# A decay-delta attention and gated MoE kernel whose table of work order is drawn anew

## The chip, the cores and the metric

The kernel runs on one core of a Trainium2 chip. The metric is device time in microseconds (us) of one execution, the median of several runs. Lower is better. The engines of a core run side by side, each strictly in the order of its own instructions: PE is TensorE (matmuls, transposes), DVE is VectorE, ACT is ScalarE, POOL is GpSimd, and SP issues the DMAs.

## The reference

The reference has two parts. A recurrent attention over 768 steps keeps one 40 x 40 state per batch (4) and head (8):

```python
y[:, :, t] = np.einsum('bhd,bhde->bhe', rt, state)
Sa = np.einsum('bhde,bhe->bhd', state, at)
state_decay = state * wt[:, :, None, :] - np.einsum('bhd,bhe->bhde', Sa, bt)
state = state_decay + np.einsum('bhd,bhe->bhde', vt, kt)
```

Its output, turned to `x` of shape (4, 768, 320), goes through `h = relu(x @ w_in)` (320 to 1024), a convolution of three taps along the sequence, `gate = sigmoid(conv)`, and `(h * gate) @ w_out` (1024 to 320). The weights arrive as 64-bit floats.

## The kernel before

**Chunks.** The 768 steps are cut into 24 chunks of 32. Inside a chunk the recurrence becomes matrix products and the inverse of a triangular system. Two neighbouring chunks (2j and 2j+1) form pair j and share their loads (`wakb`), their decays and one solve, so there are twelve solves. All four batches stand together on the 128 partitions.

**The chain of a pair.** `scores n` makes the products of the decayed rows on PE (L411, `ps`) and masks them on DVE into `at` (L437). Once both chunks of a pair have their scores, `solve_in j` takes `at` to DRAM (`bd`, L461) and back, rearranged, as `bb` (L465). `solve j` then runs 31 iterations of two operations, a product into `st` (L480) and an addition to `xx` (L486), each needing the one before. A solve of an even j runs on DVE, one of an odd j on POOL (`VSOL`). Its last step takes `xx` to DRAM (`xd`, L491) and back as `tt` (L496), which is what PE needs in the second step of `chain 2j` and of `chain 2j+1` (`pu`, L533). Only the solve's matrix goes this way; the solves of different pairs do not depend on each other, but there is one buffer each for `xx` and `bb` (two for `tt`, three for `at`), so solves run one after the other.

**The state.** `chain n` has four steps: the product with the old state on PE (`pp`, copied by ACT into `psb`), `pu` and its copy `u`, the update `pn` on PE (L549) with the addition on DVE (`s`, L562), and the scaling by the decay on POOL (L568). Chain n needs chain n-1. From the state, `u` and the turned inputs, `pairs` and `outputs` make the chunk's result, and `finish` lays it out for the second part.

**The second part.** Two chunks make a window of 64 steps; there are twelve windows. `moe_in n.fp` (four per window, ten steps each) has two halves on PE (L700), relu on ACT, the taps on ACT and DVE (L729), sigmoid, the gate, and a split into high and low parts on ACT and POOL (L743). `moe_out n.bo` (two per window) has four quarters of six matmuls (L754). `weights i` (23 pieces) turns 64-bit weights into 32-bit pairs in eight DVE operations each (L217 to L235), spread over the first third of the program.

**What sets the order.** Nothing is reordered by a scheduler. Each kind of work is a generator that gives up control after each of its steps. A long string, `ORDER`, names which work advances next, `sc21` one step of `scores 21`, `so10*2` two steps of `solve 10`, and so on. The instructions go onto their engines' queues in this order. A step whose prerequisites (`put`) have not been emitted makes them advance first:

```python
for token in ORDER.split():
    name, _, times = token.partition("*")
    ...
        advance((KINDS[name[:2]], *numbers))
```

The two-letter names are we weights, ld wakb, de decays, dd decayed, sc scores, ha hats, si solve_in, so solve, ch chain, rt/vt/ut/st turns, pa pairs, ou outputs, fi finish, pk pack, mi moe_in, mo moe_out.

Of the kernel before, what the change touches and what calls it, by code (L numbers as in the profile page):

```python
# [31 lines left out]
)  # L32

ORDER = """
    ld0 de0.0*2 ld0*2 de0.1 ld0 ld1 de0.1 we0 dd0.0*3 dd0.1*2 sc0 dd0.1 we0 ld1*2 lr0 sc0 sc1 lr1
    de1.0 sc1 ha0 de1.0 dd1.0 de1.1*2 we1*4 si0 ha0 ha1 dd1.0 we0*2 rt0 ld1 so0 ha1 dd1.0 so0 dd1.1
    ld2 so0*2 ld2 dd1.1 ld2 so0 dd1.1 ha2*2 sc2 ld2 lv0 lv1 vt0 ha3*2 so0*3 sc2 sc3 we2*2 sc3 we3
    we2*2 we3 we4 so0 we3*2 we5 we4 we5 si1 de2.0*2 ch0*4 we4*2 we6 lv2 de2.1*2 so1*2 ld3 ut0 pa0
    vt1 dd2.0*2 de3.0 we5 so1 we5 we7 ou0 we6 fi0 so1 dd2.0 ch1 we6 dd2.1 we7*2 ch1 we7 dd2.1*2 ld3
    st1*2 sc4 we6 so1 we8*4 we9 we10 ch1 lv3 rt1 we9 st1*2 ut1 pa1 lr2 ou1 ha4 ld3*2 we10 so1*3 fi0  # L40
    vt2 we10 fi0 fi1 de3.0 sc4 sc5 we9 we10 sc5 ch1 de3.1 we9 de3.1 ha4 we11 we12 lr3 rt2 fi1 st2*2
    fi1 we11 we12 we11*2 ro0 we13 we12*2 ha5 st2 we13 we14 ha5 ld4 so1 we13 dd3.0*3 dd3.1*3 we14*2
    ch2 si2 so2 ch2 pk0 ut2 so2*2 pa2 vt3 sc6 so2*2 st2 ou2 ch2 ro0 rt3 mi0.0*3 so2*2 mi0.0*2 ch2
    st3*2 we13 mi0.1*2 st3 ld4 so2 ld4 we14 lv4 we15 we16 ch3*2 sc6 sc7 ut3 we15 st3 we15 sc7 fi2*3
    lr4 mi0.0 pa3 mi0.0 ch3 we15 ch3 we16 mi0.0 we17 mi0.1 mi0.2 we17*2 mi0.2 so2 ch4 si3 we16 so3
    ou3 ha6 we16 we18 de4.0 we18 ha6 ha7 st4 fi3*2 we17 we19 de4.0 we18 mi0.1 we19 vt4 st4*3 lv5
    de4.1 ch4 ut4 so3 ch4 dd4.0 rt4 we18 we20 de4.1 we20 mi0.2 so3 we20 pa4 vt5 ch4 ch5 so3 mi0.2
    ch5 fi3 ha7 we19*2 we21*2 ut5 we20 we22*2 ou4 st5*2 mi0.1 st5 lr5 rt5 so3 we22 ld4 ld5 de5.0
    mi0.1 we21 ch5 we22 mi0.3 we21 mi0.0*2 so3 mi0.1*2 mi0.3 pa5 mi0.3 pk1 dd4.0*2 dd4.1 mi0.1*2
    dd4.1 st5 mi0.2 sc8 fi4*2 ld5 dd4.1 ou5 mi0.2 lv6 mi0.3 so3*2 sc8 mi0.2 sc9 mi0.2*2 ha8*2 ha9  # L50
    fi4 fi5 ld5 de5.0 de5.1 ha9 sc9 mi0.2 dd5.0 mi0.3 dd5.0 de5.1 lv7 mi1.0*3 mi1.1 ld5 dd5.0 dd5.1
    sc10 so3 si4 mi0.3 lr6 dd5.1*2 ch5 mi0.3 lr7 mi0.3 mi1.1*2 mi1.0*3 mi1.1 mi1.2 vt6 sc10 mi0.3
    mo0.0 sc11 mi0.3 mi1.1 mi1.0*2 mi1.1 ch6 st6 mi1.2 ch6*2 sc11 mi1.1*2 mo0.0*2 ch6 mo0.0 mo0.1*5
    ld6 ut6 rt6 ch7 mi1.1 so4 ld6 so4*2 pa6 vt7 st6 fi5*2 st6 so4*2 mi1.0 so4 mi1.2 st6 mi1.3 so4
    mi1.2 so4 lv8 ou6 mi1.0 mo1.0 mi1.2 mi1.3*2 st7*2 ch7 ut7 mi1.1 st7*2 rt7 ch7*2 mo1.0 pa7
    mi1.3*2 fi6*2 pk2 lr8 mi1.2*2 ou7 mi1.2 rt8 so4 si5 ch8 st8*2 mi1.2 mi1.3 mi1.2 mi1.3 ch8*2 lv9
    fi6 mi2.0*2 lr9 ld6 ch8 ha10*2 fi7 mi1.3*2 ha11 ld6 de6.0 vt8 lv10 de6.0 dd6.0 fi7 mi2.0 mi1.3
    mi2.1 ch9 mo1.0 mi2.0*2 de6.1 ch9 de6.1 so5*2 mi2.1 so5 mi2.0 ut8 mi2.1*4 mi2.0 mo0.0 mo1.0*2
    mo1.1 ha11 mi2.0 mi2.1 mo1.1 dd6.0 mo1.1 dd6.0 pa8 vt9 mo1.1 mi2.0*2 dd6.1 so5 fi7 st8*2 mi2.1*2
    dd6.1 so5 ou8 rt9 mi2.2 sc12 mi2.2*2 mi2.3*3 ut9 dd6.1 st9 mi2.1 mi2.2 ch9 mi2.2 mi2.3*2 mi2.2*2  # L60
    ld7 de7.0 lr10 ld7*2 so5*3 pa9 ch9 lr11 st9*3 pk3 ld7 mi2.3 mi2.2 mi3.0*2 mi2.3 mi3.0 mi2.3 fi8
    so5 fi8 mi2.2*2 mi2.3 mi3.0 ou9 mi3.1 fi8 sc12 fi9 de7.0 dd7.0 sc13 mo2.0*2 sc13 de7.1*2 mi3.1*2
    rt10 ha12*2 ha13 dd7.0 ha13 dd7.0 mi2.3 mi3.0 dd7.1*3 ch10 mi3.1*2 mi3.0 mi3.1 st10 fi9 mo2.0*2
    mo2.1 ch10*3 mo2.1 mi3.0 st10 mi3.1 st10*2 mi3.0 mi3.1 ut10 si6 so6 mi3.2*2 so6 lv11 vt10 mi3.2
    pa10 vt11 so6 mo1.1 so6 mi3.3 mo2.1 mi3.3 ch11 mo2.0 mo2.1 ld8 mi3.0 lr12 so6 ch11 so6 ou10 rt11
    mi3.3 mi3.1 ut11 pa11 st11*3 ld8 lv12 so6 mi3.2 mi3.3 st11 so6 sc14 ch11 vt12 mi3.1 lr13 sc14
    mi3.0 mo3.0 mi3.2 sc15 mi3.2 ch11 mi3.2 fi9 fi10 mi3.3 fi10*2 ou11 st12 ha14 sc15 mi3.2*2 mi3.3
    pk4 so6 ch12 mi3.2 de8.0 mi4.0*2 mi3.3 fi11*2 mi3.3 ch12*2 mo3.0 mi3.3*2 ch12 mi4.0*2 ut12 si7
# [934 lines left out]
```

## Time and profile before

| what | value |
|---|---|
| time, median of 3 runs | 711.0 us (708.99 to 714.0) |
| the profiled execution | 708.08 us |
| its span in the trace | 706.4 us (1.7 us of the time lie outside it) |
| mean granted TensorE clock | 0.906 of full speed |
| busy: PE / DVE / POOL / ACT | 560.7 / 538.4 / 353.2 / 350.7 us |

The span is cut into forty slices, whose digits are the busy tenths of each engine. A group's row gives line, engine, operation, its output and inputs, its count, its busy time and the mean of one, and how long the engine was idle ahead of it, with what ended that. A row of the timeline gives start, duration and the operation. A row of the waits gives total time, number of waits and the longest.

### The profile page before, as it was taken

What the parts mean: (1) busy time and instruction counts of PE and PEld (TensorE: products, weight loads), DVE (VectorE), ACT (ScalarE), POOL (GpSimd) and SP (SyncE); (2) the same over time, 40 slices, a digit from 0 to 9 for tenths busy, and PEclk for the clock granted to TensorE, in tenths of its full rate; (3) what the DMA queues carried; (4) which work ended last, traced back from release to release, by engine and by line L of the source; (5) the groups of instructions that cost most, each with busy time, mean ns of one, the idle gap of its engine ahead of it and who ended that gap; (6) DMA issues with size and microseconds to landing.
All of it is one profiled execution on the core that took longest, in us unless ns stands there. A gap on an engine that the chain in (4) does not pass through costs nothing. (4 is left out here: it accounts for less than half of the span.)

```text
span 706.4 us, 29930 instructions
## 1 busy us (share of the span) xinstructions
PE 560.7 (79%) x13021; PEld 497.9 (70%) x13021; DVE 538.4 (76%) x1261; ACT 350.7 (50%) x792; POOL 353.2 (50%) x582
## 2 busy tenths in 40 slices
PE   4444764677687898988977996899998977899886
PEld 3334654566576787977866885789887876788775
DVE  6689889998999896657795578987979894456571
ACT  2322244254375455664454664466565546455651
POOL 2001884037786235783234884236985028863321
PEclk9766777997799998989999998999998999999998
DMA  8765456437125344544404446524435025121000
GB/s 139 120 117 108 103 112 102 95 94 144 22 41 107 56 72 79 94 81 82 82 20 89 86 86 106 81 60 69 89 62 91 6 54 94 29 51 32 21 30 19
DMA packets 242402, 53.40 MB, mean 76 GB/s; under 512 B 229000, under 2 KB 238112, under 8 KB 242272
## 3 DMA queue, kind: packets, MB, share of 16 engines
q1 hardware_dynamic: 242272, 51.50, 39.9%
q8 instruction: 102, 1.67, 1.0%
q14 instruction: 28, 0.23, 0.1%
HBM read 38.63 MB, written 10.22 MB: 69 GB/s over the span
## 5 line engine op out<-in xcount | busy, mean ns | idle before, releaser
L729 DVE SCALAR_TENSOR_TENSOR cc<-hb,cw,cc 128x256 f32<-128x256 f32 x192 | 106.3, 575 | 13.7 <-ACT cc L721 10.2
L568 POOL TENSOR_TENSOR s<-s,wc 120x360 f32<-120x360 f32 x88 | 75.8, 891 | 69.4 <-DVE s L562 69.4
L486 POOL TENSOR_TENSOR xx<-xx,st 128x126 f32<-128x126 f32 (+22 forms) x186 | 83.1, 447 | 14.6
L480 POOL TENSOR_TENSOR st<-xx,bb 128x126 f32<-128x126 f32 (+22 forms) x186 | 79.4, 427 | 21.1 <-DMA bb<-bd 8.4
L700 PE MATMUL ph<-xh,wih 120*128 120x256 f32 x288 | 56.6, 306 | 11.3 <-ACT hb L714 11.3
L486 DVE TENSOR_TENSOR xx<-xx,st 128x126 f32<-128x126 f32 (+22 forms) x186 | 54.2, 291 | 6.4
L480 DVE TENSOR_TENSOR st<-xx,bb 128x126 f32<-128x126 f32 (+22 forms) x186 | 53.6, 288 | 7.2 <-DMA bb<-bd 1.7
L736 DVE TENSOR_TENSOR cc<-cc,hb 128x512 f32<-128x512 f32 x48 | 40.8, 857 | 21.7 <-ACT cc L734 21.5
L562 DVE TENSOR_TENSOR s<-pn,s 120x360 f32<-120x360 f32 x88 | 40.6, 522 | 20.6 <-PE pn L549 20.6
L700 PEld LDWEIGHTS ph<-xh,wih 120*128 120x128 f32 x288 | 41.8, 194 | 15.0 <-ACT hb L714 13.1
L734 ACT ACTIVATE cc<-cc 128x512 f32<-128x512 f32 x48 | 30.4, 636 | 43.6 <-DVE cc L729 43.5
L667 POOL TENSOR_TENSOR xl<-xf,xh 120x384 fp32r<-120x384 f32 x24 | 26.8, 1117 | 45.2 <-ACT xh L665 41.5
L721 ACT ACTIVATE cc<-hb,cw 128x256 f32<-128x256 f32 x96 | 43.5, 506 | 8.7 <-DVE hb L712 2.9
L602 PE MATMUL pt<-ident,s 120*120 120x120 f32 x276 | 40.6, 279 | 6.4 <-DVE s L562 3.2
L427 ACT ACTIVATE ap<-ah,hmask 120x384 f32<-120x384 f32 (+1 forms) x72 | 36.6, 576 | 17.4 <-DVE ah L391 10.1
L604 ACT COPY sn<-pt 120x360 f32<-120x360 f32 x92 | 38.9, 471 | 12.2 <-PE pt L602 11.8
L714 ACT ACTIVATE hb<-ph 128x512 f32<-128x512 f32 x48 | 28.8, 600 | 27.2 <-PE ph L700 23.4
L579 ACT ACTIVATE rp<-pr,hmask 120x384 f32<-120x384 f32 x72 | 36.7, 586 | 6.9 <-PE pr L576 6.5
L700 PE MATMUL ph<-xl,wih 120*128 120x256 f32 x192 | 39.3, 287 | 0.0
L533 PE MATMUL pu<-psb,tt 32*32 32x40 f32 x1536 | 22.5, 209 | 19.6 <-ACT psb L527 16.1
L602 PEld LDWEIGHTS pt<-ident,s 120*120 120x120 f32 x276 | 31.2, 143 | 9.0 <-DVE s L562 3.5
L533 PEld LDWEIGHTS pu<-psb,tt 32*32 32x32 f32 x1536 | 18.7, 114 | 24.5 <-ACT psb L527 17.7
(867 smaller groups left out, 1665.9 us busy)
## 6 DMA issues: line engine op xcount, KB each, us to landing
bb<-bd SPq DMA_DIRECT2D x24, 256.0 KB
w<-in_w_dram SPq DMA_DIRECT2D x24, 160.0 KB
a<-in_a_dram SPq DMA_DIRECT2D x24, 160.0 KB
k<-in_k_dram SPq DMA_DIRECT2D x24, 160.0 KB
b<-in_b_dram SPq DMA_DIRECT2D x24, 160.0 KB
r<-in_r_dram SPq DMA_DIRECT2D x96, 40.0 KB
v<-in_v_dram SPq DMA_DIRECT2D x96, 40.0 KB
out_dram<-ob SPq DMA_DIRECT2D x22, 160.0 KB
```

The lines of the kernel that those rows point to most:

```text
L480: eng.tensor_tensor(t3, xx[:, 0:nj, i : i + 1].to_broadcast([128, nj, nt]), bb[:, i : i + 1, i + 1 :].to_broadcast([128, nj, nt]), ALU.mult,)
L486: eng.tensor_tensor(xx[:, 0:nj, i + 1 :], xx[:, 0:nj, i + 1 :], t3, ALU.add)
L533: nc.tensor.matmul(pu[quad(bi), hc], tt[quad(bi), c, h, :], psb[quad(bi), hc], start=(h == 0), stop=True, skip_group_check=True,)
L562: nc.vector.tensor_tensor(new, pn[bi][:GR], old[bi], ALU.add)
L568: nc.gpsimd.tensor_tensor(n4, n4, w4, ALU.mult)
L579: nc.scalar.activation(out=rp[:, :, h, :], in_=pr[:GR], func=AF.Copy, scale=hmask[:, h : h + 1])
L602: nc.tensor.transpose(pt[:GR, g, :], old[bi][:, g, :], ident[:GR, :GR])
L604: nc.scalar.copy(sn, pt[:GR])
L700: nc.tensor.matmul(ph[:, j], l[:, fs], x, start=(j == 0 and i == 0), stop=(i == len(passes) - 1), skip_group_check=True,)
L721: nc.scalar.activation(out=cc[:, j], in_=hb[:, j, :, 1 : W + 1], func=AF.Copy, scale=cw[:, 1, f : f + 1],)
L729: nc.vector.scalar_tensor_tensor(out=cc[:, j], in0=hb[:, j, :, x : W + x], scalar=cw[:, x, f : f + 1], in1=cc[:, j], op0=ALU.mult, op1=ALU ...
L736: nc.vector.tensor_tensor(cc, cc, hb[:, :, :, 1 : W + 1], ALU.mult)
```

## The change

The string `ORDER` is replaced by another that names the same steps. Nothing else changes: every engine has the same instructions, in another order. Its last line, for an impression:

```diff
-    mi11.3*2 mi11.2*2 mo11.0 mi11.3*2 mo11.0*3 mo11.1*2 mo11.0 en0 mo11.1*2 ch23 mo11.1 en0
+    mo11.0*2 mo11.1 mo11.0 en0 mo11.1*4
```

What moves is seen on the engines. The first place is on PE, late in the program: the second step of chain 20 (`pu20`, which needs `tt10` from solve 10) and the scores of chunks 22 and 23 (`ps22`, `ps23`), which feed solve 11. The number behind a name only tells tiles apart. Before:

```order
L411 MATMUL ps22_10688<-ap22_10488,kt11_10063 32x96 x8
...
L411 MATMUL ps22_10688<-ap22_10488,bt11_10250 32x96 x8
...
L411 MATMUL ps23_10753<-ap23_10714,kt11_10063 32x96 x8
...
L411 MATMUL ps23_10753<-ap23_10714,bt11_10250 32x96 x8
...
L522 MATMUL pp20_10997<-v20_10210,at20_9854 32x40 x32
L533 MATMUL pu20_11044<-psb20_11042,tt10_10748 32x40 x32
```

Now:

```order
L754 MATMUL po70_10887<-wol_114,g72h_10348 128x320
L533 MATMUL pu20_10908<-psb20_10884,tt10_10834 32x40 x32
L754 MATMUL po70_10887<-woh_113,g73h_10708 128x320
...
L411 MATMUL ps22_11289<-ap22_11178,kt11_10753 32x96 x8
...
L411 MATMUL ps22_11289<-ap22_11178,bt11_10803 32x96 x8
...
L411 MATMUL ps23_11319<-ap23_11315,kt11_10753 32x96 x8
...
L411 MATMUL ps23_11319<-ap23_11315,bt11_10803 32x96 x8
...
L514 MATMUL pp21_11368<-s200_11093,ah10_9648 32x120
```

The scores stood 80 rows ahead of `pu20` and now stand 114 rows behind it. The same holds for pairs 0, 2, 3, 5, 6, 8 and 9: the scores of chunk 2j+3 stood ahead of `pu` of chunk 2j, and stand behind it now.

The second place is on DVE, where solve 10 begins. Before, other work stands between the second `at` of pair 10 and the solve's copy `xx10` and first product `st10_0`:

```order
L437 TENSOR_TENSOR at20_9854<-ps21_9944,trin_95 128x512
L369 SCALAR_TENSOR_TENSOR suf111_9976<-wx0_107,dsuf_102 120x384
...
L614 TENSOR_TENSOR ms18_10246<-pm18_10221,tri_89 128x512
L399 TENSOR_TENSOR bt11_10250<-pb111_10266,suf111_9976 120x6x2x32
L473 CAST xx10_10287<-xini_98 128x512
L480 TENSOR_TENSOR st10_0_10289<-xx10_10287,bb10_10024 128x31
```

Now the solve stands right behind it:

```order
L399 TENSOR_TENSOR bt10_10277<-pb101_10366,suf101_9291 120x6x2x32
L437 TENSOR_TENSOR at20_10371<-ps20_10372,trin_95 128x512
L437 TENSOR_TENSOR at20_10371<-ps21_10404,trin_95 128x512
L473 CAST xx10_10440<-xini_98 128x512
L480 TENSOR_TENSOR st10_0_10442<-xx10_10440,bb10_10435 128x31
L486 TENSOR_TENSOR xx10_10440<-xx10_10440,st10_0_10442 128x31
```

The 22 rows between them before have moved elsewhere, so `st10_0` stands two rows behind the `at` from which `bb10` is made.

More of the change, by code (lines that the diff above doesn't have):

```diff
@@ L40 @@
[L40 to L56, printed above, removed]
@@ new lines @@
+    so5*2 ld6 mi1.3 ha10*2 st8*2 ha11 ch8*4 mo1.0 mo0.1 mo1.0 lv9 ch9 mi2.1*3 fi7 so5 rt8 ha11 de6.0
+    lr9 dd6.0 fi7 mo1.0 mi2.0 mi1.3 mi2.1*2 fi7 ut8 vt8 pa8 so5 vt9 ou8 st9 de6.1 dd6.0*2 ch9*2
+    de6.1 ch9 dd6.1 mi2.2 mi2.0 mi2.2*2 mo0.0 mo1.0 mi2.3 st9*2 mi2.1*2 mi2.3 lr10 rt9 ut9 mi2.3 fi8
+    so5 st9 pa9 ou9 st10 mo1.1*4 mi2.1*2 st10*2 dd6.1 lv10 mi2.0 rt10 mi2.3 mi2.0 mi2.2*2 fi8 lv11
+    fi8 mi2.2*2 vt10 mo1.0 so5 ch10 dd6.1 mi2.3*4 ch10 mi2.2*2 mi2.3 ld7*2 de7.0 sc12 ld7 pk3
+    mi3.0*3 mi2.2 mi3.0*4 mo2.0*2 fi9 de7.0 ld7 ha12 de7.1 ha12 de7.1 ch10 mo2.0 sc12 mo1.1 mi3.1*2
@@ new lines @@
+    lr12 mi4.2 sc15 mo3.1 mi4.2 mi4.3 mi4.1 mi4.3*2 fi10 fi11 ld8 fi11 ha15 de8.0 mi4.0 ha15 mi4.0
+    de8.1*2 rt12 pa12 mo4.0 lr13 dd8.0 sc15 dd8.0 ch13 dd8.0 ou12 st13*2 mi4.2 si7 so7*4 ch13 dd8.1
+    mo3.0 fi11 vt13 fi12 mi4.2*4 mi4.1*2 mi4.2 mo4.0 ld9 mi4.2 mo4.0 dd8.1 pk5 ut13 mi5.0 fi12
+    mi4.3*2 de9.0 mi4.3*2 ld9 mi5.0 dd8.1 mi4.3 mi5.0 ld9 so7 mi5.0*3 so7 ch13*2 so7 rt13 ld9
+    mi5.1*4 st13 mi4.3*2 mo4.0*2 mi5.2 fi12 mo3.1 lv14 lv15 mi5.0*2 st13 mo4.1*2 mi5.2*2 pa13 mi5.2
+    mi5.3 sc16*2 so7*2 ch14 mo4.1 sc17*2 ou13 fi13*2 st14*3 ch14 lr14 lr15 mo4.1 mi5.1 si8 mi5.1*3
@@ new lines @@
+    mi5.3*2 mi5.0*2 mo5.0 rt14 de9.0 mi5.3 st14 vt14 dd9.0 ch14 lv16 so8 ch14 mi5.1*2 mo5.0 ch15 so8
+    de9.1 ld10 so8 de9.1 so8*2 ha16*2 mi5.2 mi5.3*2 fi13 so8 mi5.2*2 ut14 pa14 mi5.2 lr16 pk6 mo4.1
+    mi6.0*2 so8 mi6.0 mi6.1 mi5.3 vt15 ch15*2 lv17 ou14 rt15 lr17 ch15 so8 mi5.2 mi5.3*2 mi6.1
+    st15*2 ha17 mi5.2 mi6.0*2 fi14 mo5.0 fi14 mi6.0 ha17 fi14 mi6.1 dd9.0 mi5.3 mi6.0*2 ut15 mi6.2
+    pa15 vt16 so8 ch16 st15*2 ch16*2 lv18 dd9.0 de10.0 mi6.1*2 mo5.0 mo5.1 dd9.1 mo5.1 mi6.1 ld10
+    mi6.1*2 sc18 dd9.1*2 ld10 mo5.0 ou15 st16 fi15*2 ch16 ch17 mo5.1 sc18 st16 mi6.2 st16*2 mo5.1
@@ new lines @@
+    mi6.1 mi6.0 sc19*2 mi6.0 si9 so9 ld10 mi6.2 mi6.3*2 de10.0 mi6.3*2 ch17 so9*2 mi6.2*2 ut16 so9
+    fi15 pk7 so9 rt16 de10.1*2 pa16 ou16 ha18 so9 st17 so9*2 lr18 mi6.2*2 rt17 lr19 mi7.0 mi6.2
+    mi7.0*3 st17*2 fi16 st17 so9 vt17 ut17 pa17 ou17 dd10.0 mi6.1 mi6.2*2 ch17*2 st18 ch18 mi6.3
+    rt18 ch18 vt18 fi16 ld11 ut18 pa18 ha18 ch18 mi6.3*3 mi7.1*2 lr20 mi7.1*2 mi6.3*2 mi7.2 mo6.0
+    mi7.0*3 mo6.0 ha19 mo6.0 mi7.1 mi7.0 mo6.0 mo6.1 st18 mo6.0 lv19 ch18 ch19 ha19 mo6.1 mo5.1
+    dd10.0 fi16 fi17*2 ch19 mi7.2 mo6.1 st18*2 ch19 mo6.1 mi7.2*2 mi7.0 fi17 mi7.0 mi7.1 mi7.2 ou18
@@ new lines @@
+    st19 dd10.0 dd10.1 de11.0 rt19 lv20 mi7.1*2 mi7.3 mi7.2 ld11 dd10.1 mi7.3*3 mi7.2*3 ch19 mi7.1
+    vt19 sc20 dd10.1 sc20 sc21 mi7.2 sc21 si10 mi7.1 so10 fi18 so10*2 st19 pk8 mi8.0 mi7.3 ha20*2
+    mi7.3*3 ha21 mi8.0*2 mi8.1 de11.0 mi8.1 lv21 st19 mi8.1 fi18 mi8.1 ut19 st19 mi8.0 pa19 ou19
+    fi18 fi19 mi7.3 ld11 mi7.3 ha21 ld11 st20 mi8.0 mi8.1 st20*2 dd11.0*2 so10*2 mi8.0 mi8.1 so10
+    dd11.0 so10 mi8.1 so10*2 ch20 mi8.0 mo7.0*3 mo6.1 mi8.1 ch20 mo7.0 mo7.1*4 mi8.2 mi8.0*3 fi19
+    mo8.0 vt20 rt20 mi8.2 fi19 mi8.2 mi8.3 st20 mi8.2*4 de11.1*2 ch20*2 mi8.3*2 mi8.1 mi8.3 dd11.1
@@ new lines @@
+    lv23 vt23 ha23 mi10.1 mi9.3 mi10.1 mi9.3*2 mi10.1*2 ch22 ch23 st23 ch23 mi9.2 mo9.0 fi22*2 mo9.0
+    mo9.1 rt23 st23*3 mo9.1 mi10.2 mi10.0 mi10.1*3 ut23 mo9.1*2 pa23 mi10.0*3 mi10.1 ha23 mi10.1*2
+    ou23 mi10.2*2 mi10.3 ch23 mi10.3 fi22 fi23 mi10.0 fi23 mi10.0 mi10.3*2 mi10.2*3 mo10.0*2
+    mi10.3*4 mi10.2*2 mo9.0 fi23 mi10.2 pk11 mi10.3 mi11.0*3 mi10.2 mi11.0*3 ch23 mi11.0*2 mi11.1*3
+    mi11.2 mi10.3 mi11.2*3 mo10.0*2 mi11.3 mo10.1*3 mo9.1 mi11.1 mo10.1 mi11.1 mi11.0*2 mi11.1*3
+    mi11.3*2 mi11.2 mi11.3 en0 mo11.0 mi11.2 mi11.1*2 mi11.3*6 mo11.0 mi11.2*3 mo10.1 mo10.0 mi11.2
```

87 lines of the change are left out of this document (34 added, 53 removed).

## The prediction

> **What bounds the kernel now.** I read the busy shares first, then the slices.
>
> ```profile
> span 706.4 us, 29930 instructions
> PE 560.7 (79%) x13021; PEld 497.9 (70%) x13021; DVE 538.4 (76%) x1261; ACT 350.7 (50%) x792; POOL 353.2 (50%) x582
> PE   4444764677687898988977996899998977899886
> DVE  6689889998999896657795578987979894456571
> PEclk9766777997799998989999998999998999999998
> ```
>
> No engine is full. DVE leads for the first third (its slices read 8 and 9 while PE's read 4 to 7), PE after it. The kernel therefore lives on the overlap of two streams: a serial chain through the triangular solves, and matrix work that fills PE meanwhile. The second reading is whether anybody waits for the solves. The first row below is from PE's waits, the next two from DVE's and POOL's; the last four are the groups of the solve itself.
>
> ```profile
> PE pu L533 <- DMA tt<-xd: 2.7, 3, 1.8
> DVE st L480 <- DMA bb<-bd: 1.7, 1, 1.7
> POOL st L480 <- DMA bb<-bd: 8.4, 4, 5.6
> L486 POOL TENSOR_TENSOR xx<-xx,st 128x126 f32<-128x126 f32 (+22 forms) x186 | 83.1, 447 | 14.6
> L480 POOL TENSOR_TENSOR st<-xx,bb 128x126 f32<-128x126 f32 (+22 forms) x186 | 79.4, 427 | 21.1 <-DMA bb<-bd 8.4
> L486 DVE TENSOR_TENSOR xx<-xx,st 128x126 f32<-128x126 f32 (+22 forms) x186 | 54.2, 291 | 6.4
> L480 DVE TENSOR_TENSOR st<-xx,bb 128x126 f32<-128x126 f32 (+22 forms) x186 | 53.6, 288 | 7.2 <-DMA bb<-bd 1.7
> ```
>
> Almost nobody does: over twelve solves PE waits 2.7 us for `tt`, DVE and POOL 10.1 us for `bb`. The solves take (83.1 + 79.4)/6 = 27.1 us on POOL and (54.2 + 53.6)/6 = 18.0 us on DVE each, hidden beside PE's work. The length of the loop that is hidden shows in the timeline around solves 0, 10 and 11 (SPq rows are DMA issues).
>
> ```profile
> 21.43 0.69 DVE L437 TENSOR_TENSOR at<-ps,trin 128x512 f32<-128x512 f32 x1 [2.94 <-PE ps L411]
> 22.22 1.75 SPq L461 DMA_DIRECT2D bd<-at  x4
> 25.79 1.86 SPq L465 DMA_DIRECT2D bb<-bd  x2
> 32.78 0.19 DVE L480 TENSOR_TENSOR st<-xx,bb 128x31 f32<-128x31 f32 x1 [1.66 <-DMA bb<-bd]
> ...
> 375.33 1.73 SPq L496 DMA_DIRECT2D tt<-xd  x4
> 378.60 1.32 PE L533 MATMUL pu<-psb,tt 32*32 32x40 f32 x60 [0.55 <-DMA tt<-xd]
> ...
> 576.43 0.18 DVE L486 TENSOR_TENSOR xx<-xx,st 128x16 f32<-128x16 f32 x1
> 576.65 1.35 SPq L491 DMA_DIRECT2D xd<-xx  x2
> 580.59 1.88 SPq L496 DMA_DIRECT2D tt<-xd  x4
> 591.93 0.24 POOL L480 TENSOR_TENSOR st<-xx,bb 128x31 f32<-128x31 f32 x1
> 624.24 2.02 SPq L491 DMA_DIRECT2D xd<-xx  x2
> 637.26 0.84 PE L533 MATMUL pu<-psb,tt 32*32 32x40 f32 x64
> ```
>
> Four prices come out. **Hop in:** from the end of the second `at` (21.43 + 0.69 = 22.12) to the first solve operation, 10.7 us, with DVE idle for its last 1.66. **Hop out:** solve end 576.61 to the end of the `tt` issue 582.47 is 5.9 us; a `tt` whose issue ended at 377.06 let the rest of `pu` go at 378.60, 1.5 us later, together 7.4. **Back to back:** solve 10's end to solve 11's first operation, 15.3 us. **A POOL solve with its gaps:** 591.93 to 624.24 is 32.3 us, less two other POOL operations of 1.3 each, 29.7.
>
> **The change part by part.** Every instruction keeps its form and count, so no busy time is added. What moves is where the scores of chunk 2j+3, which feed solve j+1, stand against the second step of chain 2j (`pu`, L533), which needs solve j. Before, the scores stand ahead of it on PE for every j from 0 to 10: solve j+1 is fed while solve j still runs. Now they stand behind it for j = 0, 2, 3, 5, 6, 8, 9, 10. Both engines run strictly in their order, so there hop in, solve, hop out and a stretch of PE work follow one another. I price PE work by the busy time of one line over the whole span; rows in order: L700 (96 half steps of moe_in, 1.17 each), L754 (100 quarters of moe_out, 1.03), L638 (outputs), L411 (48 scores and pairs, 1.27), L549 (23 state updates, 1.95), L533 (24, 0.94).
>
> ```profile
> 0.00:706.40 706.40, 112.00 (x768) 99.06 (x768) 0.91 0.41 76
> 0.00:706.40 706.40, 103.02 (x600) 89.14 (x600) 0.91 0.41 76
> 0.00:706.40 706.40, 39.25 (x3072) 34.91 (x3072) 0.91 0.41 76
> 0.00:706.40 706.40, 60.94 (x2304) 51.39 (x2304) 0.91 0.41 76
> 0.00:706.40 706.40, 44.81 (x1104) 38.53 (x1104) 0.91 0.41 76
> 0.00:706.40 706.40, 22.47 (x1536) 18.65 (x1536) 0.91 0.41 76
> ```
>
> Example: between `pu` of chunk 20 and the scores of chunk 23 there now stand seven quarters of moe_out (7.2), four halves of moe_in (4.7), and of the attention one state update, one pairs, two scores, one outputs and nine transposing steps of about half a us each (together 14.1): 26.0 us. The other stretches are worked out alike. While solve j runs, the order puts before the next `pu` only 10.8 to 58.1 us of PE work, 33.8 on average, against 14.9 to 101.5 and 58.1 before.
>
> Other work stands inside the solve on the solving engine: weight conversions (eight operations), the gate's L729, state updates L562 and L568. It is counted by these rows (a conversion from the first to the last of the two timeline rows, 27.59 to 30.32, 2.7 us; a gate's four L729 4 x 575 ns; L562 4 x 522; L568 4 x 891).
>
> ```profile
> L729 DVE SCALAR_TENSOR_TENSOR cc<-hb,cw,cc 128x256 f32<-128x256 f32 x192 | 106.3, 575 | 13.7 <-ACT cc L721 10.2
> L562 DVE TENSOR_TENSOR s<-pn,s 120x360 f32<-120x360 f32 x88 | 40.6, 522 | 20.6 <-PE pn L549 20.6
> L568 POOL TENSOR_TENSOR s<-s,wc 120x360 f32<-120x360 f32 x88 | 75.8, 891 | 69.4 <-DVE s L562 69.4
> 27.59 0.29 DVE L217 TENSOR_SCALAR wi10q<-wi10r 120x256 int32<-120x256 int32 x1
> 29.90 0.42 DVE L235 TENSOR_TENSOR wi10q<-wi10q 120x256 f32<-120x256 f32 x1
> ```
>
> The path, turn by turn (us; even solves on DVE at 18.0, odd ones on POOL at 29.7):
>
> | solve | into it | solve + other work in it | hop out | work until the next feed |
> |---|---|---|---|---|
> | 0 | 10.7 | 18.0 + 10.5 | 7.4 | 43 |
> | 1 | in the 43 | 29.7 + 2.5 | beside | none |
> | 2 | 15.3 | 18.0 + 17.2 | beside | 34 (DVE) |
> | 3 | 10.7 | 29.7 + 11.8 | 7.4 | 14 |
> | 4 | 10.7 | 18.0 + 23.3 | beside | none |
> | 5 | 15.3 | 29.7 + 13.3 | 7.4 | 30 |
> | 6 | in the 30 | 18.0 + 0.6 | 7.4 | 36 |
> | 7 | 10.7 | 29.7 + 11.6 | 7.4 | 10 |
> | 8 | in the 10 | 18.0 + 11.7 | 7.4 | 19 |
> | 9 | 10.7 | 29.7 + 1.5 | 7.4 | 38 |
> | 10 | 10.7 | 18.0 + 15.3 | 7.4 | 26 |
> | 11 | 10.7 | 29.7 + 6.8 | 7.4 | 76 (to the end) |
>
> The 43 are 18 to the scores of chunk 3 (9.6 us of PE work with a handshake at each of some six small steps) and about 25 until POOL gets past an operation that waits for ACT and for conversions now ahead of it; it is the least certain entry, from about 25 to 50. The 34 are 31 us of DVE rows, and a little contention. The tail was 706.4 - 637.3 = 69.1 us from solve 11's first `pu` (row above), and some 7 us more PE work stands behind it now.
>
> The start, up to the second `at`, was 22.12 us; some 30 us of DVE work stands ahead of it now instead of some 18, five weight conversions among it instead of one, and these need their loads from the same queue: I take 41 (from 32, DVE work without gaps, to 45). That conversions are brought forward also saves later DVE time, but DVE then waits for a solve anyway; I count nothing for it.
>
> Sum: start 41 + hops in 7 x 10.7 = 74.9 + 2 x 15.3 = 30.6 + solves 6 x 18.0 + 6 x 29.7 = 286.2 + other work in them 126.1 + hops out 9 x 7.4 = 66.6 + the work between 250 + tail 76 = 951.4. The profiled run took 708.08 us for a span of 706.4, 1.7 outside, which gives **953 us**. That run stands 2.9 under the median of 711.0, which is within the spread of the three (708.99 to 714.0).
>
> **A rule against it, and the clock.** Where PE is left idle for long now, its granted clock is low (columns: PE busy, PEld, DVE, ACT, POOL, then clock).
>
> ```profile
> 0.00:25.00 25.00, 14.36 (x144) 11.89 (x144) 16.31 (x39) 8.10 (x16) 3.81 (x17) 1.00 0.77 135
> 25.00:50.00 25.00, 6.64 (x31) 5.52 (x30) 20.42 (x69) 5.20 (x14) 1.59 (x2) 0.62 0.77 129
> 50.00:75.00 25.00, 13.40 (x341) 11.45 (x340) 23.66 (x65) 7.20 (x18) 6.60 (x13) 0.64 0.55 102
> 475.00:500.00 25.00, 24.44 (x456) 22.76 (x448) 19.69 (x37) 16.15 (x37) 19.39 (x30) 1.00 0.39 72
> ```
>
> With PE busy 6.64 of 25 us the clock was 0.62, with 24.44 it was 1.00. The Trainium skill, "TensorE: Matmul & The Clock Gate", section "What's actually happening", says that after an idle window of about 3.4 us PE falls to half its clock until it has been busy for as long again. The two rows agree in direction. By that rule the sum would be higher, since each turn now holds an idle wait of 15 to 25 us; it is a rival below.
>
> **The rivals.**
> - *The cold clock.* Each wait throttles PE, and the stretches between solves (about 170 us of the 250 are PE work, plus the start) run at 0.62 to 0.8. At 1.3 times, 210 us become 273: **1016 us**. For it, the rows above; against it, half of these stretches is handshakes with ACT and DVE, which no clock sets.
> - *Partial overlap.* Hops are shorter when the queue of SP is empty, and PE's stretch drains while the solve is late for another reason, so that half of the 245 us that I add stays hidden: **830 us**. For it: the walk adds up terms that a real order could let overlap by two engines' slack. Against it: on PE the `pu` blocks all that stands behind it.
> - *Nothing.* Sums of work, which are unchanged (PE 560.7, DVE 538.4), set the time, and each stream catches up: **711 us**. For it: PE has 146 us of idle time that could take waits. Against it: the waits add some 250.
> - *The other side, faster.* DVE is idle 8.7, 4.6 and 1.3 us in the first three windows above, 14.6 in all, and the change brings conversions there. If it fills this idle time and no solve is waited for later, **696 us**. It decides if PE's wait for `tt` stays under 15 us in all.
>
> **How the numbers follow.** Forecast 0.66, cold clock 0.12, partial overlap 0.15, nothing 0.03, faster 0.04. The forecast's own terms (start 32 to 45, the 43 as 25 to 50, hops by 1 us each, prices by some 5%) span about 900 to 1005. The range reaches to both large rivals: 830 to 1035. About 1% is what a measurement of this kernel can tell from no change; faster by more 0.04, within it 0.03, slower 0.93.
>
> **What would show it.** In the profile of the changed kernel: PE's wait at `pu` for `tt` should be near 150 us or more over about ten waits, against 2.7; the first L480 on DVE and POOL should wait for `bb` in most turns; PE's slices should show a dip in each of twelve turns, with a lower clock in the dips; solve 11 should end near 870 us. I am wrong if `pu` seldom waits for `tt` (then scores were fed early in spite of their place), if the turns are shorter than about 60 us, or if the start takes far more than 45 us.

## The result: 1138 us against 712, 1.60 times as long

| | before | changed |
|---|---|---|
| time, median of 4 runs each | 711.8 us | 1138.1 us (1134.6 to 1141.6) |
| ratio | | 1.599, 95% interval 1.592 to 1.607 |
| span of the profiled run | 706.4 us | 1139.8 us |
| granted TensorE clock | 0.906 | 0.750 |

The forecast was 953 us with a range of 830 to 1035. The direction is right and the size is not: 1138 lies outside the range, and the loss is 426 us where 242 were forecast.

The head of the page of the changed kernel, with the busy shares and the slices:

```profile
span 1139.8 us, 29896 instructions
PE 656.9 (58%) x13021; PEld 572.3 (50%) x13021; DVE 507.8 (45%) x1261; ACT 354.8 (31%) x792; POOL 319.7 (28%) x582
PE   3317436463753746878284573774864736638764
DVE  7665516882315622465753338532233634123342
PEclk9557656676767787889597687797787667769976
```

The counts of each engine are those of before. PE's slices now go up and down through the whole span, and often one engine is low where the other is high: in slices 20 and 25 PE reads 2 and 3 and DVE 7 and 8, in slices 27 and 29 PE 7 and 8 and DVE 3 and 2. The engines take turns. PE is busy 96 us longer for the same 13021 matmuls at the lower clock; DVE and POOL are busy for less time than before.

The waits of the solve, one row each of PE's, DVE's and POOL's waits in the changed kernel:

```profile
PE pu L533 <- DMA tt<-xd: 20.3, 4, 16.2
DVE st L480 <- DMA bb<-bd: 37.4, 4, 10.9
POOL st L480 <- DMA bb<-bd: 68.0, 5, 24.6
```

`bb` is now waited for 105.4 us instead of 10.1, and `tt` 20.3 instead of 2.7. That is 113 us more, as much as a quarter of the loss, though waits of different engines are not simply a part of it. Many other waits have grown too, of which the prediction did not speak. The groups of the page show them (the last column is the idle time ahead of the group):

```profile
L729 DVE SCALAR_TENSOR_TENSOR cc<-hb,cw,cc 128x256 f32<-128x256 f32 x192 | 102.1, 554 | 70.0 <-ACT cc L721 66.4
L568 POOL TENSOR_TENSOR s<-s,wc 120x360 f32<-120x360 f32 x88 | 70.0, 828 | 144.1 <-DVE s L562 144.1
L562 DVE TENSOR_TENSOR s<-pn,s 120x360 f32<-120x360 f32 x88 | 40.6, 524 | 64.3 <-PE pn L549 64.3
L714 ACT ACTIVATE hb<-ph 128x512 f32<-128x512 f32 x48 | 28.9, 602 | 104.3 <-PE ph L700 74.3
L716 DVE COPY hend<-hb 128x16 f32<-128x16 f32 x48 | 11.5, 248 | 103.9 <-ACT hb L714 103.3
```

Before, the idle time ahead of these five was 13.7, 69.4, 20.6, 27.2 and 16.6 us. For the last two the rows of before are:

```profile
L714 ACT ACTIVATE hb<-ph 128x512 f32<-128x512 f32 x48 | 28.8, 600 | 27.2 <-PE ph L700 23.4
L716 DVE COPY hend<-hb 128x16 f32<-128x16 f32 x48 | 12.4, 264 | 16.6 <-ACT hb L714 16.5
```

These are hand-overs of the second part and of the state chain. Most are 3 to 5 us long on average, with single ones of up to 20 us; POOL's twelve at L568 are 12 us on average.

One turn, from the second `at` of pair 10 to the `pu` that needs solve 11 (timeline; DVE, SPq, PE and POOL rows):

```profile
874.44 0.69 DVE L437 TENSOR_TENSOR at<-ps,trin 128x512 f32<-128x512 f32 x1 [2.94 <-PE ps L411]
875.05 0.42 DVE L473 CAST xx<-xini 128x512 f32<-128x512 bf16 x1
884.16 0.19 DVE L480 TENSOR_TENSOR st<-xx,bb 128x31 f32<-128x31 f32 x1 [8.70 <-DMA bb<-bd]
...
921.90 1.34 SPq L491 DMA_DIRECT2D xd<-xx  x2
925.55 1.72 SPq L496 DMA_DIRECT2D tt<-xd  x4
927.67 1.11 PE L533 MATMUL pu<-psb,tt 32*32 32x40 f32 x6 [16.19 <-DMA tt<-xd]
...
971.12 0.69 DVE L437 TENSOR_TENSOR at<-ps,trin 128x512 f32<-128x512 f32 x1 [2.10 <-PE ps L411]
981.50 0.24 POOL L480 TENSOR_TENSOR st<-xx,bb 128x31 f32<-128x31 f32 x1 [24.61 <-DMA bb<-bd]
1031.35 0.80 PE L533 MATMUL pu<-psb,tt 32*32 32x40 f32 x64
```

It is the turn that was forecast: DVE idle 8.70 us for `bb` right behind the `at`, PE idle 16.19 us for `tt`, then the `at` that the scores of chunk 23 give, some 43 us later, and POOL idle for the next `bb`.

All twelve turns can be read off in this way. The columns are those of the forecast, in us:

| solve | into it | solve and work in it | hop out | until the next feed |
|---|---|---|---|---|
| 0 | 9.2 | 26.1 | 12.6 | 44.5 |
| 1 | in the 44.5 | 31.6 | beside | none |
| 2 | 16.8 | 37.8 | beside | 36.9 |
| 3 | 9.0 | 59.6 | 9.6 | 15.4 |
| 4 | 9.2 | 46.8 | beside | none |
| 5 | 17.0 | 51.6 | 22.2 | 39.4 |
| 6 | in the 39.4 | 22.8 | 9.2 | 38.7 |
| 7 | 11.1 | 38.9 | 18.3 | 17.2 |
| 8 | in the 17.2 | 39.2 | 12.9 | 25.2 |
| 9 | 9.9 | 29.5 | 8.8 | 59.5 |
| 10 | 9.1 | 37.7 | 5.8 | 44.1 |
| 11 | 9.7 | 40.6 | 9.2 | 108.5 (to the end) |

With the start of 38.6 they add up to the span of 1139.8. The turns have the forecast shape, and their sum says where the 188 us beyond the forecast span are: solves +50, hops out +42, the work between +71, the tail +32, the rest -7. Such a sum tells where time passes. Whether it passes there because of the loop is another question, and the experiments answer it differently.

### The profile page after: what moved, and what is told of

The parts are those of the page before. It is cut to its first block, busy times and chain, and to the rows that moved or that the text cites. A ratio compares the mean times of both kernels' runs of the same rounds, so it can differ in the third digit from the quotient of the medians.

```text
span 1139.8 us, 29896 instructions
## 1 busy us (share of the span) xinstructions
PE 656.9 (58%) x13021; PEld 572.3 (50%) x13021; DVE 507.8 (45%) x1261; ACT 354.8 (31%) x792; POOL 319.7 (28%) x582
## 5 line engine op out<-in xcount | busy, mean ns | idle before, releaser
L729 DVE SCALAR_TENSOR_TENSOR cc<-hb,cw,cc 128x256 f32<-128x256 f32 x192 | 102.1, 554 | 70.0 <-ACT cc L721 66.4
L568 POOL TENSOR_TENSOR s<-s,wc 120x360 f32<-120x360 f32 x88 | 70.0, 828 | 144.1 <-DVE s L562 144.1
L480 POOL TENSOR_TENSOR st<-xx,bb 128x126 f32<-128x126 f32 (+22 forms) x186 | 68.9, 370 | 81.2 <-DMA bb<-bd 68.0
L486 POOL TENSOR_TENSOR xx<-xx,st 128x126 f32<-128x126 f32 (+22 forms) x186 | 71.8, 386 | 14.6
L700 PE MATMUL ph<-xh,wih 120*128 120x256 f32 x288 | 67.2, 351 | 12.5 <-ACT hb L714 12.5
L480 DVE TENSOR_TENSOR st<-xx,bb 128x126 f32<-128x126 f32 (+22 forms) x186 | 52.7, 283 | 43.1 <-DMA bb<-bd 37.4
L562 DVE TENSOR_TENSOR s<-pn,s 120x360 f32<-120x360 f32 x88 | 40.6, 524 | 64.3 <-PE pn L549 64.3
L602 PE MATMUL pt<-ident,s 120*120 120x120 f32 x276 | 47.8, 309 | 28.4 <-POOL s L568 17.7
L736 DVE TENSOR_TENSOR cc<-cc,hb 128x512 f32<-128x512 f32 x48 | 34.1, 719 | 58.3 <-ACT cc L734 58.0
L700 PEld LDWEIGHTS ph<-xh,wih 120*128 120x128 f32 x288 | 51.2, 235 | 16.9 <-ACT hb L714 14.6
L700 PE MATMUL ph<-xl,wih 120*128 120x256 f32 x192 | 45.8, 326 | 23.2 <-POOL xl L667 23.1
L716 DVE COPY hend<-hb 128x16 f32<-128x16 f32 x48 | 11.5, 248 | 103.9 <-ACT hb L714 103.3
L514 PE MATMUL pp<-s,ah 120*32 120x120 f32 (+1 forms) x552 | 33.0, 308 | 42.5 <-POOL s L568 23.7
L734 ACT ACTIVATE cc<-cc 128x512 f32<-128x512 f32 x48 | 30.2, 631 | 85.3 <-DVE cc L729 85.3
L486 DVE TENSOR_TENSOR xx<-xx,st 128x126 f32<-128x126 f32 (+22 forms) x186 | 51.5, 277 | 6.4
L602 PEld LDWEIGHTS pt<-ident,s 120*120 120x120 f32 x276 | 36.1, 159 | 31.2 <-POOL s L568 18.3
```

The source lines that it names most:

```text
L480: eng.tensor_tensor(t3, xx[:, 0:nj, i : i + 1].to_broadcast([128, nj, nt]), bb[:, i : i + 1, i + 1 :].to_broadcast([128, nj, nt]), ALU.mult,)
L486: eng.tensor_tensor(xx[:, 0:nj, i + 1 :], xx[:, 0:nj, i + 1 :], t3, ALU.add)
L562: nc.vector.tensor_tensor(new, pn[bi][:GR], old[bi], ALU.add)
L568: nc.gpsimd.tensor_tensor(n4, n4, w4, ALU.mult)
L602: nc.tensor.transpose(pt[:GR, g, :], old[bi][:, g, :], ident[:GR, :GR])
L700: nc.tensor.matmul(ph[:, j], l[:, fs], x, start=(j == 0 and i == 0), stop=(i == len(passes) - 1), skip_group_check=True,)
```

## The experiments

Theory A is that of the prediction: the late feeds make solve and matrix work take turns, and everything else follows. Its rivals were drawn up on seeing the waits above: the order is worse in many places by itself, in the second part (M), in the queues of DVE and POOL behind the solves (Q), or locally everywhere (L). In the first four runs these rivals stand together as theory B. Where a run changes only the table, the instructions stay the same. "Sequence in the same slots" means that the places in the table that held a step of the named kinds still do, and only which of these steps comes first, second and so on is exchanged.

### Cutting the loop

```diff
 def solve_in(pd):
+    if j:
+        pd["bb"] = pds[0]["bb"]; yield; return
 def solve(pd, cuts):
     ...  # the 31 iterations stay
+    if j:
+        pd["tt"] = pds[0]["tt"]; yield; return
```

Later solves and chains so read what pair 0 made, and wait for nothing; the transfers of pairs 1 to 11 are gone with the dependences. In the new table:

> The new table with the loop cut: from pair 1 on, the solves read the bb of pair 0 and the chains read the tt of pair 0, so the bounces through DRAM of pairs 1 to 11 are left out and no chain waits for a solve and no solve for scores. All vector work of the solves stays. The result is not the reference's. Theory A: about 740 us (700 to 790), since without the loop the work is the same as before. Theory B (short distances, late loads): 850 to 950, what is left over 711 is theirs. The cold clock has no cause of its own here by A.

Measured: 1041.0 us (ratio to before 1.469, 1.465 to 1.473). In the old table:

> The table of before with the same cut of the loop (bounces of pairs 1 to 11 left out, solves kept). The result is not the reference's. Theory A and B: the loop was hidden before, so little is won, 685 to 711 us. If it falls below 660, the loop was a bound before as well.

Measured: 703.3 us (0.9935, 0.990 to 0.997). The loop was hidden before, as the prediction said. But without it the new table still takes 338 us more than the old. **Theory A as stated falls**: it gave 740. Theory B's 850 to 950 was too low as well. The loop, its dependences and transfers together, is worth 97 us in the new table.

### Leaving the solves out

```diff
 def solve(pd, cuts):
+    if j:  # besides the cut: none of the 31 iterations
+        for _ in cuts: yield
+        yield
+        pd["tt"] = pds[0]["tt"]; yield; return
```

> The new table with the loop cut as before and the vector work of solves 1 to 11 left out too (twelve solves of 18.0 us on DVE and 27.1 on POOL become one). The result is not the reference's. Theory Q (with the loop cut, solves still cost since steps that the chain needs stand behind them in the queues of DVE and POOL; 189 us of solve work lie on the chain of the run with the loop cut): 840 to 900 us. Theory L (many short distances; solves only fill waits that are there anyway): 950 to 1030 us.

Measured: 919.5 us (1.293, 1.285 to 1.300).

> The table of before with the same left out. The result is not the reference's. The solves lie beside PE's work, but DVE is the bound in the first third: 640 to 690 us by both. It is the base against which the run of the new table without solves is read.

Measured: 684.4 us (0.963, 0.959 to 0.967). Nothing waited for the solves' results any more, yet their vector work still held 121 us in the new table and 19 in the old. What stands behind it in the queues of DVE and POOL comes later, and others wait for that. Two rows with the loop cut, PE's wait for POOL's scaling of the state and ACT's wait for the taps on DVE, then the same two without solves (total, number, longest):

```profile
PE pp L547 <- POOL s L601: 19.9, 9, 12.3
ACT cc L767 <- DVE cc L762: 85.1, 30, 12.5
```

```profile
PE pp L554 <- POOL s L608: 7.3, 13, 1.9
ACT cc L774 <- DVE cc L769: 63.7, 30, 4.8
```

The lines of these kernels are shifted by their edits: the rows are L514 and L568, L734 and L729 of before. POOL's own idle time ahead of that scaling says nothing here: it grew from 133.3 to 186.3 us when the solves were left out, as POOL had less to do. So Q holds in part, 919.5 lying between the two forecasts. And 235 us of difference between the tables (919.5 less 684.4) are left when neither the solves' waits nor their work are there.

### Repairing and breaking the feeds

One place in the new table, then with the scores of pair 11 ahead of the end of solve 10 and the steps of solve 11 spread:

```diff
-so10*2 ch20 mi8.0 mo7.0*3 mo6.1 mi8.1 ch20 mo7.0 ... sc22 sc23*2 mi8.2 si11 so11 ch21*2 so11*2
+sc22 dd11.1*2 sc22 sc23*2 so10*2 si11 ... ch20 mi8.0 mo7.0*3 mo6.1 mi8.1 ch20 mo7.0 mo7.1 so11
```

> The new table with one thing repaired: the scores of chunks 2j+2 and 2j+3 (with the loads and decays they need) are emitted ahead of the last step of solve j, solve_in j+1 right behind solve j, and the eight steps of solve j+1 spread evenly over the stretch up to its old end. The second part of the kernel and the other steps stay in the new order. Theory A (turn taking: late feeds put hop in, solve, hop out and PE work one behind another, and everything else follows from that): the path loses the seven hops in and the stretches of PE work, some 300 us, about 800 us, between 730 and 870. Theory B (the new order has short distances between producer and consumer everywhere, so small waits add up whatever the solves do): at least 1000 us. A plus cold clock alone: 850 to 900.

Measured: 1093.6 us (1.543, 1.538 to 1.549), 45 won. That is theory B's number. But this repair has a flaw of its own: spread over the stretch, solves 1 to 11 became 38 to 80 us long and followed one another closely, so a new wait probably took the place of the old one. It says little on A.

The converse, in the old table:

```diff
-so10 sc23 si11 pa19 ... ch20*2 mi8.1*3 ch20*2 mo8.0*2 ... so11*2
+so10 ... ch20*2 mi8.1*3 ch20*2 mo8.0*2 ... mi8.3*3 mi9.0 sc23 si11 so11*5
```

> The table of before with only the fault of the new one put in: for j = 0, 2, 3, 5, 6, 8, 9, 10 the second step of scores 2j+3 is held back until as many steps behind the second step of chain 2j as in the new table, and what needs it (solve_in, solve j+1, some decayed) waits with it. Theory A: most of the loss returns. Eight turns pay hop in and hop out (18 us each, 145) and the PE stretch (some 180), less the slack of about 10 us per turn that the old turns had: some 900 us, between 820 and 1000. Theory B: the scores' place alone does little, 711 to 780.

Measured: 858.7 us (1.211, 1.206 to 1.216). This is within theory A's range and far from B's. The late feeds alone cost 150 us in an order that is good otherwise. That mechanism of the prediction is shown, with about a third of the loss.

### The second part's sequence

```diff
-ch20 mi8.0 mo7.0*3 mo6.1 mi8.1 ch20 mo7.0 mo7.1*4 mi8.2 mi8.0*3 fi19
+ch20 mi8.0*2 mi8.1*2 mo7.1 mi8.1 ch20 mi8.1 mi8.0*3 mo7.1*2 mi8.0*2 mo7.0 fi19
```

> The new table in which only the steps of the second part (pack, moe_in, moe_out, end) are put in the sequence that they have among themselves in the table of before, in the same slots; attention, loads and weights stay in the new order. Theory M (the new order of the second part, with producers next to their consumers, holds PE and DVE up): most of the 330 us that are left without the loop go, 800 to 900 us. Theory Q (the attention's steps on DVE and POOL stand behind solves and other work in their queues): little changes, 1050 to 1140 us.

Measured: 1068.2 us (1.509, 1.498 to 1.521).

```diff
-fi18 fi19*3 mi8.0 mo7.1*2 mi8.0*2 mo7.0 ch20*2 mi8.1*3 ch20*2
+fi18 fi19*3 mo7.1*2 mi8.2 mi8.0*3 ch20*2 mo8.0 mi8.2*2 ch20*2
```

> The converse: the table of before with the second part's steps in the sequence of the new table, in the old slots. Theory M: 850 to 1000 us. Theory Q: 700 to 780 us. If neither this nor its converse moves the time, the second part's own order is out as a cause.

Measured: 875.3 us (1.238, 1.228 to 1.247). Put into the good table, the new sequence costs 168 us (against 707.6 beside it); taken out of the bad one, it gives back 70. Neither theory's numbers for the pair came out together: M is right on one side, Q on the other. That fits faults that fill the same waits.

### Both at once

The two edits of the feeds and of the second part together, first as repair of the new table, then as fault in the old:

```diff
-(new table)  +(scores early, solves spread; mi, mo, pk, en in the old sequence)
-(old table)  +(scores late; mi, mo, pk, en in the new sequence)
```

> The new table with both repairs: scores fed early and solves spread, and the second part's steps in the sequence of before. If the late feeds and the second part are the two causes, each covering for the other: 720 to 850 us. If the rest of the attention's order (chain, turns, loads, weights) is the larger cause: about 1000 us, the single gains of 45 and 70 us added up.

Measured: 1018.6 us (1.434, 1.429 to 1.439), the forecast of the case that the rest of the attention's order is the larger cause. The repair of the feeds has its flaw here too: solves 1 to 11 are 36 to 68 us long.

> The table of before with both faults: scores 2j+3 late by as many steps as in the new table, and the second part's steps in the sequence of the new table. If they add up, 150 + 167 over 708, about 1025 us. If they fill the same waits, 880 to 920 us. 1138 would mean that these two are the whole change.

Measured: 978.0 us (1.376, 1.371 to 1.380), between the two forecasts. Two faults bring 267 us of the 426, less than the 318 that their single costs add up to. Two repairs bring 120, about the sum of 45 and 70. The two are not the whole change: 160 us are missing in the run with both faults.

### How local the loss is

The new table cut into stretches, each sorted as in the old one; one place for 83 and for 20 steps:

```diff
-sc20 dd10.1 sc20 sc21 mi7.2 sc21 si10 mi7.1 so10 fi18 so10*2 st19 pk8
+sc20*2 sc21 de11.0 mi7.1 sc21 ha20 si10 ha20 ha21 mi7.1 ha21 dd11.0*2 ... so10*2   # 83
+sc20*2 sc21 mi7.1 sc21 si10 mi7.1 mi7.2*3 pk8 so10*2 st19 mi8.0 so10              # 20
```

> The new table cut into stretches of 83 steps (half a pair's work); inside each the steps stand in the order of before, the stretches hold the same steps as in the new table. It repairs what is local and part of the late feeds (six of the nine pairs whose scores came late get them early). Theory L (many short distances between producer and consumer): 750 to 850 us. Theory that the cause lies in a displacement over more than half a pair: above 950.

Measured: 883.5 us (1.247, 1.239 to 1.255).

> The same with stretches of 20 steps (an eighth of a pair's work). The late feeds stay (seven of eight). Theory L: a good part of the loss goes although the feeds stay late, 850 to 980 us. Theory A or Q, for which the stretches of solve and chain over tens of steps decide: 1050 to 1140 us.

Measured: 1103.8 us (1.557, 1.547 to 1.567). Sorting over half a pair's work gives back 255 us, over an eighth of it 34. The first lies between the forecasts, and a part of its 255 is that feeds come early again: by the place of the scores on PE, those for pairs 0, 2, 3 and 5, four of the eight (the expectation counted six of nine). With 20 steps all eight stay late, and 1103.8 is as forecast for A or Q. Theory L in its strict form, neighbours that stand too close, falls: the displacements that matter reach over more than 20 steps, and many lie within 83.

### Without solves: which steps hold the other 235 us

All these runs leave loop and solves out, and exchange sequences between the tables in the same way. First the second part:

```diff
-(new table, no solves)  +(mi, mo, pk, en in the old sequence)
-(old table, no solves)  +(mi, mo, pk, en in the new sequence)
```

> The new table without loop and solves (919.5 us), and with the second part's steps in the sequence of before. The result is not the reference's. On the chain of the run without solves, moe_in takes 198 us against 118 in the old table without solves, and the hand-over gaps 72 against 37. Theory M (the second part's steps on DVE, ACT and POOL stand too close behind one another): 800 to 840 us. If the attention's own steps are the larger part of the 235 us that are left: 880 to 910.

Measured: 856.0 us (1.208, 1.201 to 1.214), between the two forecasts.

> The old table without loop and solves (684.4 us), with the second part's steps in the sequence of the new table. The result is not the reference's. Theory M: 780 to 830 us, so the new sequence costs 100 to 150 by itself where no solve is in its way. If its cost in the run with solves (167 us) came only from its meeting the solves on DVE and POOL: 690 to 720.

Measured: 787.0 us (1.109, 1.103 to 1.114), as theory M had it. So the second part's sequence costs 64 to 103 us with no solve in its way; at 168 with solves, a third or so of its cost came from meeting them. The waits that grow are DVE's, first of the old table without solves, then with the new sequence (here too the lines are shifted: L776 and L777 are the gate's product, L736 of before; `hend` is the copy of the edge columns, L716; L769 and L770 are the taps, L729):

```profile
DVE cc L776 <- ACT cc L774: 24.6, 20, 5.8
DVE hend L756 <- ACT hb L754: 20.6, 12, 5.7
DVE cc L769 <- ACT cc L761: 13.0, 13, 3.1
```

```profile
DVE hend L757 <- ACT hb L755: 53.3, 19, 6.4
DVE cc L770 <- ACT cc L762: 53.0, 18, 7.5
DVE cc L777 <- ACT cc L775: 21.9, 25, 3.8
```

DVE's waits for ACT in moe_in go from 58.2 to 128.2 us. The longest single wait is 7.5 us: it is many small waits, each for a relu, a first tap or a sigmoid that ACT has not finished. In the tables, the median distance from a moe_in's second half on PE, with its relu, to the copy of its edge columns on DVE (`hend`) is 6.5 steps in the old, 3 in the new and 3.5 in this exchange. That these 70 us of waits are the bulk of the 103 is likely, but no run shows it by itself.

Then the steps of the chain:

```diff
-(new table, no solves)  +(ch, rt, vt, ut, st, pa, ou, fi, ha, lv, lr in the old sequence)
```

> The new table without loop and solves (919.5 us), with the steps of chain, turns, pairs, outputs, finish, hats and the loads of v and r in the sequence of before, in the same slots. The result is not the reference's. By the chain of the run without solves (chain 127 us against 81, loads of v 14 against 0, turns and pairs some 25 more): 840 to 870 us. If these only shift the wait to the second part's steps: 890 to 920.

Measured: 890.2 us (1.253, 1.246 to 1.260), 29 us less: as forecast if the exchange only shifts the wait, and not the sum over the chain.

Last, all sequences at once against the pattern in which three groups take turns:

```diff
-(new table, no solves)  +(old sequence inside each of three groups, new pattern)
-(old table, no solves)  +(new sequence inside each of three groups, old pattern)
```

> Without loop and solves. The steps are sorted into three groups: the second part; chain, turns, pairs, outputs, finish, hats and loads of v and r; and loads, decays, scores, solves and weights. Inside each group the steps stand in the old sequence, while the pattern by which the groups take turns is that of the new table. The result is not the reference's. If the sequences inside the groups hold the rest of the loss: 700 to 760 us. If the pattern by which the groups take turns holds it: 800 to 850.

Measured: 803.7 us (1.130, 1.123 to 1.136), as forecast for the pattern.

> The converse without loop and solves: inside the groups the new sequences, the pattern of the old table. The result is not the reference's. If the sequences inside the groups hold the loss: 860 to 920 us. If the pattern holds it: about 790, little over the run with the second part alone exchanged.

Measured: 909.7 us (1.281, 1.274 to 1.287), as forecast for the sequences. The new sequences under the old pattern have nearly all the loss (225 of 235); the old sequences under the new pattern have half of it (119). The sequences inside the groups are nearly enough to cause it, and the pattern can cause half where the sequences are good. In both runs over a hundred of the 1999 steps had to be emitted earlier than the pattern asked, since something needed them, so this split is rough.

## Why the prediction was wrong, and what of it was right

- **Direction and the loop.** Scores behind the `pu` of the pair before make hop in, solve, hop out and PE work follow one another. The run with late feeds in the old table shows it at 150 us, and the 105 us of waits for `bb` show it in the trace. The hops in came out at 9.0 to 11.1 us (forecast 10.7), the two solves back to back at 16.8 and 17.0 (15.3); these terms were good to a few us. The start was 38.6 (41). One reading was off: that before "solve j+1 is fed while solve j still runs". The scores did run on PE then, but the second `at` of pair 11 ended at 577.21 us, 0.6 behind the end of solve 10, and in ten of the eleven turns it ended up to 10 us behind the solve. The old order hid the loop since its feed did not wait for `pu`.
- **The step that failed: PE's price as the wall time of a stretch.** "I price PE work by the busy time of one line over the whole span" took a stretch between two solves as long as its PE work. Three of the four longest stretches (behind solves 9, 10 and 11), in the changed kernel (span, then PE busy; the clock is the third figure from the end):

```profile
815.60:875.10 59.50, 41.13 (x763) 37.04 (x763) 24.22 (x44) 23.86 (x53) 14.34 (x14) 0.79 0.13 25
927.70:971.80 44.10, 31.05 (x568) 26.94 (x571) 13.24 (x28) 14.66 (x32) 7.07 (x8) 0.76 0.05 15
1031.30:1139.80 108.50, 73.77 (x1037) 64.93 (x1036) 37.46 (x80) 39.62 (x85) 21.71 (x20) 0.84 0.07 18
```

  The forecasts were 38, 26 and 76. PE is busy 41, 31 and 74 us there, so the PE work was sized well, 3 to 5 us more at the lower clock in the first two. Behind solves 3, 5, 6, 7 and 8 it was too: PE is busy 13, 34, 34, 10 and 19 us, forecast 14, 30, 36, 10 and 19. What was left out is PE's idle time, 18, 13 and 35 us in the three rows: hand-overs inside the second part and the chain, most of them (14, 9 and 18 us) waits for ACT. These three stretches are 72 us longer than forecast, of the 188. In the old order more steps stand between the two sides of such a hand-over, as at `hend` above. I carried the prices of that order over to one without the cover.
- **The same omission in the other terms.** A solve and the work inside it were taken at their own durations: 412 us in all, measured 462. The solves themselves, short gaps included, take 287 us where 286 were forecast, by luck: 119 against 108 on DVE and 169 against 178 on POOL. The other work takes 114 (126 forecast). The remaining 61 us are waits inside the solve, for ACT, PE and the other of DVE and POOL. The hop out was 7.4 us forecast and 12.1 on average. Behind solves 0 and 5 (12.6 and 22.2 us) PE waited 11.6 and 5.1 us for `psb`, which ACT makes and which `pu` needs beside `tt`. Behind solve 7 (18.3 us), which ended at 654.57, eight loads of v stood ahead of `xd` in SP's queue, so `xd` was issued 9.1 us after the solve's end; in the turn of solve 10 it was 0.03 us:

```profile
655.31 8.28 SPq L336 DMA_DIRECT2D v<-in_v_dram  x8
663.68 1.34 SPq L491 DMA_DIRECT2D xd<-xx  x2
667.33 2.71 SPq L496 DMA_DIRECT2D tt<-xd  x4
```

- **The cause of the whole.** "Every instruction keeps its form and count, so no busy time is added", and what moves is the place of the scores: by this the prediction put all of the loss on the loop, and that is refuted. With the loop cut 338 us of difference were left, with the solves out 235. The prediction weighed one set of places in a table of 1999 steps, and took the order of the rest as neutral. The new sequence of the second part alone costs 168 us in the old table, more than the late feeds (150). PE's busy time, too, did not stay: it rose by 96 us.
- **Signs named.** The first L480 waited for `bb` in nine turns, the slices dip in every turn, and the clock is lower: right. PE's wait for `tt` "near 150 us" was 20.3: wrong, since PE, idle for 483 us in all (146 before), stands still at other steps of the turn before it gets to `pu`. Solve 11 ended at 1022 us, not at 870.
- **The rivals.** "Nothing" and "faster" fail by the direction, and "partial overlap" erred to the wrong side. "Cold clock" had its sign right: the clock fell to 0.750 and PE's busy time rose by 96 us. How much of that is on the path was not tested by a run; following the chain of waits back over the whole span (and on from the instruction that ended last where it breaks off), PE's own work on it is 288 us before and 314 after. At the mean slowing of 656.9/560.7 = 1.17 the clock's part of these 314 would be some 46 us; that is an estimate. The Trainium skill's page "TensorE: Matmul & The Clock Gate", section "What's actually happening", says that idle time throttles PE; these traces agree, 0.906 against 0.750.

What stays open: which of the 1999 steps hold the 160 us that are missing in the run with both faults, and, without solves, the 100 to 140 us of the 235 that neither the second part's nor the chain's sequence alone accounts for. The faults overlap, and single exchanges cannot add up to the whole.

## What to carry to other kernels

Where several engines run strictly in the order of one table, a change of that table must be priced at every hand-over between engines, above all at the many short ones, and a stretch of work lasts as long as its engine is busy only if other work covers its waits. A sum of stages that fits a trace says where the time passes; taking a dependence away says whether it is the cause: here that took 97 us of 426. And faults in an order can hide each other: put each alone into the good order (150 and 168 us here) rather than only repairing it in the bad one (45, with a repair that brought a wait of its own, and 70).

## What the runs showed of the hardware

- The solve on POOL is faster where DVE has less to do. L480 on POOL took 370 ns on average in the changed kernel against 427 before, L486 386 against 447, with DVE busy 45% of the span instead of 76%; on DVE the same operations went from 288 to 283 and from 291 to 277 ns. The trace of before shows it inside one kernel, with the same shapes compared (the mean over the shapes): L480 on POOL took 349 ns on average where DVE was busy for less than a tenth of the operation's time (50 operations) and 468 where it was busy for over seven tenths (125); L486 took 371 and 473 (45 and 117). Which of DVE's operations slow it was not tried.

```profile
L480 POOL TENSOR_TENSOR st<-xx,bb 128x126 f32<-128x126 f32 (+22 forms) x186 | 68.9, 370 | 81.2 <-DMA bb<-bd 68.0
L486 POOL TENSOR_TENSOR xx<-xx,st 128x126 f32<-128x126 f32 (+22 forms) x186 | 71.8, 386 | 14.6
```

- The same matmuls kept PE busy 560.7 us at a mean clock of 0.906 and 656.9 at 0.750; without solves it was 550.9 at 0.915 in the old table and 620.7 at 0.817 in the new. The busy time of PE is no measure of work between two kernels whose waits differ.
